# Placing TensorE's bursts in a fused attention and MoE kernel: empty sequencer instructions instead of split matmuls

## The chip, the cores and the metric

The kernel runs on one core of a Trainium2 chip. The metric is the device time of one execution in microseconds: the kernel before takes 282.03 us, the median of three runs (281.68 to 282.23).

## The reference

Two layers follow each other. The first is a linear attention with cosine weights over 8 batches, 8 heads, 576 positions and 64 columns a head; the second is a gated layer over the 4608 tokens that come out of it.

```python
# attention: q, k, v are [8, 8, 576, 64]
theta = pi / 2 * arange(576) / 576
phi(x) = concat([relu(x) * cos(theta), relu(x) * sin(theta)])     # 128 features
kv  = einsum('bhsf,bhfd', phi(k), v);  z = phi(k).sum(over positions)
x   = (phi(q) @ kv) / (phi(q) @ z + 1e-6)          # -> [4608, 512], heads side by side
# second layer: w_in [512, 2048], w_out [2048, 512], beta [2048]
h   = x @ w_in
out = (h * sigmoid(beta * h)) @ w_out
```

All inputs and the output are float32 in memory; the kernel's matmuls take bfloat16 and sum in float32.

## The kernel before

The attention is computed batch by batch (8 batches, b = 0 to 7), the second layer by chunks of 512 tokens (9 chunks, c = 0 to 8). While chunk c is in the second layer, batch c + 1 goes through the attention, in the gaps of the same program. The instructions of every engine are in the order in which the source gives them.

The attention of one batch has two stretches on TensorE that are made of many tiny matmuls. One is kv, 72 matmuls (L272 of the profile). The other is the numerators, 144 matmuls of 64 rows, 64 columns and 65 moved columns (L293). This text calls the second kind a burst. Each of TensorE's matmuls is a pair of instructions, a weight load and the matmul itself, so a burst is 288 instructions.

```python
def num_mm(b, n, jp, bank, slot):
    for cs in range(2):
        for jj in range(2):
            rows = slice(jj * HP, (jj + 1) * HP)
            for g in range(2):
                cols = slice(g * HP, (g + 1) * HP)
                nc.tensor.matmul(ps[cols, bank + jj, slot * E : (slot + 1) * E],
                                 lhsT=(qts[b % 2], qs_of(b))[cs][rows, jp, n, cols],
                                 rhs=kv[rows, g, jp, cs, :], start=(cs == 0), stop=(cs == 1))

def num_all(b, t, bank):            # three of these make one burst
    for i in range(3):
        for jp in range(2):
            num_mm(b, 3 * t + i, jp, bank, 2 * i + jp)
```

In the second layer, chunks 0 and 1 use plain products. From chunk 2 on the output, and from chunk 5 on also half of h, is computed by a scheme with seven products of half-size blocks instead of eight (names 1 to 7 in the code); it needs sums and differences of blocks of the operands, which VectorE makes. For h these are sums of weights (made once) and sums of x (made for each chunk):

```python
def x_sums(c):
    xt, n = xt_tile(c), NB // 2
    X11, X12, X21, X22 = (xt[:, i * n : (i + 1) * n, jp] for jp in range(2) for i in range(2))
    t1, t2, t3, t4 = (wx["x"][:, i] for i in range(4))
    nc.vector.tensor_tensor(t1, X12, X11, op=ALU.subtract)       # L458
    nc.vector.tensor_tensor(t2, X22, t1, op=ALU.subtract)        # L459
    nc.vector.tensor_tensor(t3, X22, X12, op=ALU.subtract)       # L460
    nc.vector.tensor_tensor(t4, X21, t2, op=ALU.subtract)        # L461
```

In three places a matmul can be split by columns into two of half the width, which computes the same and makes TensorE's program longer by two instructions. The splits serve nothing but that: they shift where in the program the bursts begin.

```python
def h_plain(c, jt, bank, cols=1):                     # plain half of h, chunks 5 to 8
    xt = xt_tile(c)
    w = NB // cols
    for mi in range(MI):                              # MI = 4
        jp, g = divmod(mi, 2)
        for o in range(0, NB, w) if mi else (0,):     # the first of four is never split
            z = o + w if mi else NB
            nc.tensor.matmul(ps[:, bank, o * 64 : z * 64], lhsT=win[...], rhs=xt[:, o:z, jp, ...], ...)

def o_mm(c, tt, jts, cols=1):                         # output of chunks 0 and 1
    ...
    for jt in jts:
        w = DM // cols if jt > 0 else DM              # jt = 0 is never split
        for m0 in range(0, DM, w):
            nc.tensor.matmul(o_ps[:, m0 : m0 + w], lhsT=gs[c, jt // 4][...], rhs=wout[:, jt, m0 : m0 + w], ...)

# inside o_fast: one of the seven products of the output, chunks 2 to 8
def prod(dst, left, right, start, stop, pieces=False):
    for i in order:                                   # 8 matmuls of 256 columns
        w = HM // 2 if i and pieces else HM
        for m in range(0, HM, w):
            nc.tensor.matmul(dst[:, m : m + w], lhsT=left(i), rhs=right[:, i, m : m + w], ...)
```

Which are split: in chunk 1's output those from slot 24 on (slots 16 to 31 are four parts of four matmuls for each of four groups of tokens); in chunk 5's output product 4 of the first half of the tokens and products 2, 5, 7, 3, 4 of the second; in chunk 6 all eight groups of `h_plain`.

The end of chunk 4, with the second half of its output (`y`), stands in the source like this. `v_half` scales v for the next batch; its fifth argument is the engine, VectorE if there is none. The digits are products on TensorE, `a2`, `a7`, `a3` additions on VectorE, `c1`, `c5`, `cu`, `c4` copies on ScalarE.

```python
        y["1"]()
        ...
        v_half(b + 1, 0, 0, 3)
        y["5"]()
        y["c5"]()
        v_half(b + 1, 1, 2, 3, "act")
        y["6"]()
        y["cu"]()
        y["2"]()
        y["a2"]()
        v_half(b + 1, 0, 3, 5)
        y["7"]()
        y["a7"]()
        v_half(b + 1, 0, 5, 7)
        y["3"]()
        y["a3"]()
        v_half(b + 1, 0, 7, 9)
        if c == FAST - 1:                 # FAST = 5
            x_sums(c + 1)
        v_half(b + 1, 1, 3, 9, "act")
        y["4"]()
        y["c4"]()
```

Product 4 adds to the block of PSUM that `a7` reads, so it waits for `a7`. Chunk 5 begins with `ORDER = "Y1 c1Y X5 X1 ..."`: Y1 is two matmuls on x itself, X5 the first product on a sum of x (t1), X1 again one on x. The numerators are the letter N, late in that order and after all products of h.

Of the kernel before, what the change touches and what calls it, by code (L numbers as in the profile page):

```python
# [22 lines left out]
def kernel(  # L23
# [14 lines left out]
    nc = tc.nc  # L38
# [145 lines left out]
    def xt_tile(c):  # L184
        if c not in xts:
            xts[c] = xt_pool.tile([P, NB, 2, P], BF16, name="xt", tag="xt")
        return xts[c]
# [33 lines left out]
    def tan_mul(eng, dst, src, n0, n1):  # L221
        return eng.tensor_tensor(  # L222
            dst.rearrange("q n (g p) -> q n g p", g=2), src.rearrange("q n (g p) -> q n g p", g=2),
            tanr[:, n0:n1].unsqueeze(2).to_broadcast([P, n1 - n0, 2, HP]), op=ALU.mult)
# [23 lines left out]
    def qs_of(b):  # L248
        return wx["q"] if b > 3 and b % 2 == 0 else qs_first
# [5 lines left out]
    def q_tan(b, jp, behind=None):  # L255
        got = tan_mul(nc.gpsimd, qs_of(b)[:, jp], qts[b % 2][:, jp], 0, NQ)

        if behind is not None:
            tc.add_manual_dep(got.ins, behind.ins.name,
                              mybir.DependencyInfo(mybir.DependencyClass.Sync, mybir.DependencyReason.DATA),  # L260
                              reason="GpSimd behind the sums")
# [66 lines left out]
    def num_all(b, t, bank):  # L328
# [81 lines left out]
    def h_group(c, jt):  # L410
        h_mm(c, jt)
        h_act(c, jt)

    def h_silu(c, jt, bank):
        if (c, jt // 4) not in gs:
            gs[c, jt // 4] = gt_pool.tile([P, 4, TCH], BF16, name="g_t", tag="g_t")
        nc.scalar.activation(gs[c, jt // 4][:, jt % 4], ps[:, bank], AF.Silu, scale=beta[:, jt : jt + 1])  # L417

    def h_plain(c, jt, bank, cols=1):
        xt = xt_tile(c)  # L420
        w = NB // cols
        for mi in range(MI):
            jp, g = divmod(mi, 2)
            for o in range(0, NB, w) if mi else (0,):
                z = o + w if mi else NB
                nc.tensor.matmul(ps[:, bank, o * 64 : z * 64], lhsT=win[jt // 4][:, mi, (jt % 4) * P : (jt % 4 + 1) * P],  # L426
                                 rhs=xt[:, o:z, jp, g * HP : (g + 1) * HP],
                                 start=(mi == 0), stop=(mi == MI - 1 and z == NB))
# [101 lines left out]
    def o_part(c, tt, part, cols=1):  # L530
        o_mm(c, tt, range(4 * part, 4 * part + 4), cols)
# [226 lines left out]
    def v_half(b, cs, n0=0, n1=NQ, eng="dve"):  # L758
        if b >= B:
            return  # L760
        v_scale(b, cs, n0=n0, n1=n1, eng=eng)
        if cs == 1 and n1 == NQ and b + 1 < B:
            load_raw(b + 1, "v")
# [11 lines left out]
    def x_part(b, t, bank):  # L775
        x_div(t, bank)
        x_turn_dma(b, 3 * t, 3 * t + 3)
# [51 lines left out]
    for slot in range(32):  # L829
        if slot < 16:  # L830
            h_group(1, slot)
        else:
            o_part(1, (slot - 16) // 4, slot % 4, 2 if slot > 23 else 1)
        one_unit(slot)

    def k_piece(b, j):
# [20 lines left out]
    H_COLS, O_COLS = {6: 8}, {5: ("4", "25734")}  # L857

    def x_sum(c, kind):
        xt, n = xt_tile(c), NB // 2  # L860
# [24 lines left out]
    def chunk(c, b, x, y, parts):  # L885
        steady = {"X": (0, 2, 0, 1), "Y": (4, 3, 4, 5), "Z": (8, 0, 2, 1), "V": (12, 4, 3, 5)}
        end = {"X": (0, 6, 0, 1), "E": (2, 5, 3, 4), "Y": (4, 2, 0, 1), "F": (6, 7, 3, 4), "Z": (8, 6, 0, 1),
               "V": (12, 5, 3, 4)}
        pairs = {n: h_fast(c, at[0], at[1:]) for n, at in (steady if b < B else end).items()}

        def plain_bank(n):
            return (2 if n == 7 else 6 + n % 2) if b < B else (2, 7)[n % 2]

        plain = [2, 3, 6, 7, 10, 11, 14, 15]
        outs = {"x": x, "y": y}

        def q_next():
            if b + 2 < B:
                q_turn_dma(b + 2)
                if b + 3 < B:  # L900
                    load_raw(b + 3, "q")

        def raw_next(name):
            if b + 2 < B:
                load_raw(b + 2, name)

        xs_all = {"x0", "x1", "x2"}
        take = prep(b, [
            ({"k0", "k1", "k2", "k3"} | xs_all, lambda: raw_next("k")),
            ({"q0", "q1"} | xs_all, q_next),  # L910
            ({f"{o}{n}" for o in "vw" for n in range(NQ)}, lambda: raw_next("v"))])
        last_sum = None
        for op in (ORDER if b < B else ORDER_END).split():
            n = int(op[-1]) if op[-1].isdigit() else None
            if op == "K":
                kv_mm(b, 0, 4)
                kv_mm(b, 1, 4)
            elif op == "kt":
                kv_take((0, 1), 4)
            elif op[0] == "N":  # L920
                for t, bank in enumerate(parts):
                    num_all(b, t, bank)
            elif op[0] == "x":
                x_part(b, n, parts[n])
                take(op)
            elif op[0] in "kvwq":
                take(op)
            elif op[0] == "t":
                if c + 1 < NTC:
                    x_sum(c + 1, n)  # L930
            elif op[0] == "g":
                if b + 1 < B:
                    q_tan(b + 1, n, None if n else last_sum)
            elif op[0] == "p":
                h_plain(c, plain[n], plain_bank(n), 2 if n < H_COLS.get(c, 0) else 1)
            elif op[:2] == "sp":
                h_silu(c, plain[n], plain_bank(n))
            elif op[0] == "o" and n is not None:
                outs[op[1]][op[2]]()
            elif op[0] == "o":  # L940
                outs[op[2]]["a" + op[1]]()
            elif op[0] == "c" and op[2] in "xyo":
                outs["x" if op[2] == "o" else op[2]][op[:2]]()
            elif op[0] == "s":
                last_sum = g_sum(c, 2 * int(op[1]), 2 * int(op[1]) + 2, n)
            else:
                pair = op[0] if op[0] in pairs else op[-1]
                pairs[pair][op.replace(pair, "")]()
# [24 lines left out]
    FAST = 5  # L973
    for c in range(2, NTC):
        b = c + 1
        parts = (6, 0, 4) if c < FAST else (0, 6, 4)
        cols = O_COLS.get(c, ("", ""))
        xb, yb = ((2, 3, 6), (1 if c == FAST - 1 else 7, 3, 6)) if c < FAST else ((3, 2, 0), (1, 2, 0)) if b < B else ((0, 3, 6), (1, 3, 6))
        x, y = o_fast(c, 0, xb, cols[0]), o_fast(c, 1, yb, cols[1])
        if c >= FAST:  # L980
            chunk(c, b, x, y, parts)
            continue
        sums = h_first(c)
        for t, bank in enumerate(parts):
            num_all(b, t, bank)
        q_tan(b + 1, 0, sums)
        q_tan(b + 1, 1)
        for i, n in enumerate("156273"):
            x[n]()
            if n in "156":  # L990
                x["c" + ("u" if n == "6" else n)]()
                x_part(b, i, parts[i])
        for j in range(4):
            k_piece(b + 1, j)
        for n in ("a7", "a2", "a3"):
            x[n]()
        att_q(b + 2)
        y["1"]()
        y["c1"]()
        v_half(b + 1, 1, 0, 1, "act")  # L1000
        x["4"]()
        x["c4"]()
        v_half(b + 1, 1, 1, 2, "act")
        v_half(b + 1, 0, 0, 3)
        y["5"]()
        y["c5"]()
        v_half(b + 1, 1, 2, 3, "act")
        y["6"]()
        y["cu"]()
# [6 lines that stand above are left out]
        y["3"]()  # L1016
        y["a3"]()
        v_half(b + 1, 0, 7, 9)
        if c == FAST - 1:
            x_sums(c + 1)  # L1020
        v_half(b + 1, 1, 3, 9, "act")
        y["4"]()
        y["c4"]()
# [30 lines left out]
```

## Time and profile before

| engine | busy us | share of the span |
|---|---|---|
| TensorE, matmuls | 272.2 | 97% |
| TensorE, weight loads (beside matmuls) | 192.4 | 69% |
| VectorE | 209.1 | 75% |
| ScalarE | 177.8 | 64% |
| GpSimd | 71.9 | 26% |

The profiled execution has a span of 279.6 us and 8687 instructions; TensorE's clock is at full speed throughout. The costliest lines of TensorE are L544 (products of the output, chunks 2 to 8), L378 (h of chunks 0 to 4), L521 (output of chunks 0 and 1), L426 (plain half of h, chunks 5 to 8) and L472 (products of h, chunks 5 to 8).

How to read it: matmuls are pipelined, so the length of one in the profile is longer than its share of TensorE's time; the time that a matmul takes from the engine is the difference between its start and the next one's. Busy shares say which engine is full. Idle time of an engine and its releaser say what it waited for, and "issue" means that the profile shows nothing it waited for. A queue of the kind "instruction" carries program text to an engine.

### The profile page before, as it was taken

How to read it: one execution, taken by the hardware profiler on the slowest of the kernel's cores; microseconds unless marked ns; L12 is line 12 of the kernel's file. 1: busy time of each engine (PE TensorE's matmuls, PEld its weight loads, DVE VectorE, ACT ScalarE, POOL GpSimd, SP SyncE). 2: the span in 40 equal slices, each digit the busy share in tenths (PEclk: the TensorE clock that was granted, in tenths of full speed). 3: DMA queues.
4: the chain of work that ended last, by engine and by line, in shares of the span. 5: the costliest groups of instructions: out<-in, count | busy, mean ns of one | idle time of the engine just before them, and what ended most of it. 6: DMA issues, size and time to landing. Idle time of an engine off the chain costs nothing.

```text
span 279.6 us, 8687 instructions
## 1 busy us (share of the span) xinstructions
PE 272.2 (97%) x3592; PEld 192.4 (69%) x3592; DVE 209.1 (75%) x539; ACT 177.8 (64%) x348; POOL 71.9 (26%) x89
## 2 busy tenths in 40 slices
PE   8999999999999999999999999999999999999993
PEld 8564455455674588548854886679888886888783
DVE  5989967669999586357749977799679779649832
ACT  5778756772137557675757585896685179529911
POOL 1444000633194074106320542007400140000000
PEclk9999999999999999999999999999999999999999
DMA  7999999999979959992899289407400540033006
GB/s 243 373 394 385 391 390 323 348 244 397 164 233 330 293 151 249 182 340 41 196 193 374 61 205 250 177 12 115 116 1 7 122 113 1 2 79 74 0 2 150
DMA packets 50583, 53.98 MB, mean 193 GB/s; under 512 B 31200, under 2 KB 31472, under 8 KB 50544
## 3 DMA queue, kind: packets, MB, share of 16 engines
q1 hardware_dynamic: 47584, 45.82, 58.0%
q0 software_dynamic: 2688, 7.34, 9.2%
q8 instruction: 28, 0.46, 0.7%
q10 hardware_dynamic: 272, 0.27, 0.4%
q14 instruction: 11, 0.09, 0.2%
HBM read 36.71 MB, written 9.44 MB: 165 GB/s over the span
## 4 chain that ended last, share of the span: by engine, by line
PE 89%; DMA 5%; DVE 3%; issue 1%; ACT 0%; ACTq 0%
PE ps L544 30%; PE ps L378 22%; PE ps L472 11%; PE ps L521 8%; PE ps L426 7%; DMA raw_q<-in_q_dram 5%; PE ps L293 4%; PE ps L272 3%; PE ps L602 1%; PE ps L234 1%; PE ps L606 1%; DVE xs L315 1%; DVE vb L219 0%; PE ps L616 0%; PE ps L352 0%
## 5 line engine op out<-in xcount | busy, mean ns | idle before, releaser
L378 PE MATMUL ps<-xt,win 128*128 128x512 bf16 (+1 forms) x324 | 71.1, 377 | 0.1
L386 ACT ACTIVATE g_t<-ps,beta 128x512 bf16<-128x512 f32 x80 | 54.6, 688 | 19.2 <-PE ps L378 17.9
L378 PEld LDWEIGHTS <-win 128*128 128x128 bf16 x324 | 31.1, 98 | 35.4 <-issue 0.2
L514 POOL DMA_DIRECT2D out_dram<-o_sb x56 | 32.7, 590 | 66.6 <-DVE o_sb L595 34.3
L544 PEld LDWEIGHTS <-S 128*128 128x128 bf16 x469 | 44.2, 98 | 4.8
L417 ACT ACTIVATE g_t<-ps,beta 128x512 bf16<-128x512 f32 x64 | 41.2, 696 | 3.4 <-PE ps L426 2.2
L544 PEld LDWEIGHTS <-g_t 128*128 128x128 bf16 x357 | 32.9, 98 | 3.7
L222 POOL TENSOR_TENSOR qs<-qt,tanr 128x1152 bf16<-128x1152 bf16 x8 | 18.9, 2387 | 48.5 <-DVE S L397 17.6
L397 DVE TENSOR_TENSOR S<-g_t 128x512 bf16<-128x512 bf16 (+1 forms) x62 | 22.3, 393 | 11.5 <-ACT g_t L386 9.1
L521 PE MATMUL ps<-wout,g_t 128*128 128x512 bf16 (+1 forms) x158 | 29.2, 339 | 0.0
L544 PE MATMUL ps<-wout,g_t 128*128 128x256 bf16 (+1 forms) x231 | 28.1, 270 | 0.0
L544 PE MATMUL ps<-wout,S 128*128 128x256 bf16 (+1 forms) x238 | 27.4, 266 | 0.0
L544 PE MATMUL ps<-T,S 128*128 128x256 bf16 (+1 forms) x231 | 27.1, 269 | 0.0
L426 PE MATMUL ps<-xt,win 128*128 128x512 bf16 (+1 forms) x120 | 24.0, 336 | 0.0
L315 DVE TENSOR_TENSOR xs<-ps,rden 128x768 bf16<-128x768 f32 (+4 forms) x26 | 22.8, 883 | 0.8
L219 DVE TENSOR_SCALAR vb<-raw_v,cos 128x256 bf16<-128x256 f32 x63 | 22.9, 421 | 0.2 <-DMA raw_v<-in_v_dram 0.2
L521 PEld LDWEIGHTS <-g_t 128*128 128x128 bf16 x158 | 15.0, 98 | 11.0
L217 ACT ACTIVATE vb<-raw_v,sin 128x256 bf16<-128x256 f32 (+1 forms) x50 | 21.8, 499 | 0.8 <-DMA raw_v<-in_v_dram 0.8
L472 PE MATMUL ps<-w_stage 128*128 128x256 bf16 x120 | 20.3, 273 | 0.4 <-DVE w_stage L458 0.4
L472 PEld LDWEIGHTS <-w_stage 128*128 128x128 bf16 x160 | 15.5, 98 | 4.2 <-issue 0.5
L222 POOL TENSOR_TENSOR w_stage<-qt,tanr 128x1152 bf16<-128x1152 bf16 x4 | 9.5, 2380 | 26.1 <-DVE den L304 26.1
L426 PEld LDWEIGHTS <-win 128*128 128x128 bf16 x120 | 11.7, 98 | 6.3
(104 smaller groups left out, 384.9 us busy)
## 6 DMA issues: line engine op xcount, KB each, us to landing
raw_v<-in_v_dram SPq DMA_DIRECT2D x7, 1152.0 KB, 10.9
raw_k<-in_k_dram SPq DMA_DIRECT2D x7, 1152.0 KB, 8.4
raw_q<-in_q_dram SPq DMA_DIRECT2D x7, 1152.0 KB, 7.8
out_dram<-o_sb POOLq DMA_DIRECT2D x56, 128.0 KB, 5.2
w_stage<-in_moe_w_in_dram SPq DMA_DIRECT2D x3, 1024.0 KB, 13.3
w_stage<-in_moe_w_out_dram SPq DMA_DIRECT2D x2, 1024.0 KB, 8.4
w_stage<-in_moe_w_out_dram SPq DMA_DIRECT2D x4, 512.0 KB, 12.0
out_dram<-o_sb SPq DMA_DIRECT2D x13, 128.0 KB, 2.4
```

The lines of the kernel that those rows point to most:

```text
L219: nc.vector.tensor_scalar(o, a, scalar1=t[:, n : n + 1], scalar2=None, op0=ALU.mult)
L222: return eng.tensor_tensor(dst.rearrange("q n (g p) -> q n g p", g=2), src.rearrange("q n (g p) -> q n g p", g=2), tanr[:, n0:n1].unsqueez ...
L315: nc.vector.tensor_tensor(o.rearrange("q j n s d -> q j (n s) d"), nv[:, :, a:z, :, 0:D].rearrange("q j n s d -> q j (n s) d"), rden[:, :, ...
L378: nc.tensor.matmul(ps[:, h_bank(c, jt), blocks.start * 64 : blocks.stop * 64], lhsT=win[jt // 4][:, mi, (jt % 4) * P : (jt % 4 + 1) * P], ...
L386: nc.scalar.activation(gs[c, jt // 4][:, jt % 4], ps[:, h_bank(c, jt)], AF.Silu, scale=beta[:, jt : jt + 1])
L397: return nc.vector.tensor_tensor(o, l, r, op=op)
L417: nc.scalar.activation(gs[c, jt // 4][:, jt % 4], ps[:, bank], AF.Silu, scale=beta[:, jt : jt + 1])
L426: nc.tensor.matmul(ps[:, bank, o * 64 : z * 64], lhsT=win[jt // 4][:, mi, (jt % 4) * P : (jt % 4 + 1) * P], rhs=xt[:, o:z, jp, g * HP : (g ...
L472: nc.tensor.matmul(dst, lhsT=left[:, g], rhs=right[:, :, g * HP : (g + 1) * HP], start=start and g == 0, stop=stop and g == 1, skip_group_ ...
L514: eng.dma_start(out=out_v[bb, n][:, m0:m1], in_=o_sb[hf * HP : (hf + 1) * HP, m0:m1])
L521: nc.tensor.matmul(o_ps[:, m0 : m0 + w], lhsT=gs[c, jt // 4][:, jt % 4, tt * P : (tt + 1) * P], rhs=wout[:, jt, m0 : m0 + w], start=(jt == ...
L544: nc.tensor.matmul(dst[:, m : m + w], lhsT=left(i), rhs=right[:, i, m : m + w], start=start and i == 0, stop=stop and i == order[-1], skip ...
```

## The change

It has three parts. First, the splits in chunks 5 and 6 go, and in their place 137 empty instructions (nops) are put into TensorE's program ahead of chunk 5; a nop computes nothing and takes one place in the program where a split matmul adds two. Second, chunk 1's output is split from slot 19 on, not from slot 24. Both are for the places at which the bursts begin. Third, the four sums of x for chunk 5 are given earlier in chunk 4, so that they are there when chunk 5 asks for them. What is computed stays the same. The table PADS holds two counts for a chunk, ahead of the chunk and after its burst; only the first of chunk 5 is not zero.

```diff
+    def pad(c, n):
+        for _ in range(PADS.get(c, (0, 0))[n]):
+            nc.tensor.nop(hint="pad", nofuse=True)
...
-            o_part(1, (slot - 16) // 4, slot % 4, 2 if slot > 23 else 1)
+            o_part(1, (slot - 16) // 4, slot % 4, 2 if slot > 18 else 1)
...
-    H_COLS, O_COLS = {6: 8}, {5: ("4", "25734")}
+    PADS = {5: (137, 0)}
...
-                h_plain(c, plain[n], plain_bank(n), 2 if n < H_COLS.get(c, 0) else 1)
+                h_plain(c, plain[n], plain_bank(n))
...
     for c in range(2, NTC):
         ...
-        cols = O_COLS.get(c, ("", ""))
+        pad(c, 0)
         ...
-        x, y = o_fast(c, 0, xb, cols[0]), o_fast(c, 1, yb, cols[1])
+        x, y = o_fast(c, 0, xb), o_fast(c, 1, yb)
...
         y["5"]()
         y["c5"]()
+        if c == FAST - 1:
+            x_sums(c + 1)
         v_half(b + 1, 1, 2, 3, "act")
...
         v_half(b + 1, 0, 7, 9)
-        if c == FAST - 1:
-            x_sums(c + 1)
         v_half(b + 1, 1, 3, 9, "act")
```

(Left out: a second call of `pad` after the numerators, which places nothing with this table.)

More of the change, by code (lines that the diff above doesn't have):

```diff
@@ L922, in chunk @@
                     num_all(b, t, bank)
+                pad(c, 1)
             elif op[0] == "x":
@@ L985 @@
             num_all(b, t, bank)
+        pad(c, 1)
         q_tan(b + 1, 0, sums)
```

## The prediction

> **What bounds the kernel now.** I read the busy shares first, then the chain that ended last, then who waited on TensorE, then the timeline at the places where TensorE stood still. Shares and chain of the page:
>
> ```profile
> PE 272.2 (97%) x3592; PEld 192.4 (69%) x3592; DVE 209.1 (75%) x539; ACT 177.8 (64%) x348; POOL 71.9 (26%) x89
> ...
> PE 89%; DMA 5%; DVE 3%; issue 1%; ACT 0%; ACTq 0%
> ...
> q8 instruction: 28, 0.46, 0.7%
> ```
>
> TensorE is 97% busy and 89% of the chain, so nothing on another engine counts unless TensorE waits for it. The third line is the queue that brings TensorE its program: 28 packets, 0.46 MB, 16 KB each. I need it below.
>
> The waits of TensorE alone come to three microseconds (columns: who waited for whom, us in total, times, longest). The first, third and fifth lines lie in the first 20 us, which the change does not touch:
>
> ```profile
> PE ps L602 <- DVE zero_b L149: 1.0, 1, 1.0
> PE ps L293 <- issue: 0.9, 2, 0.5
> PE ps L293 <- ACT kv L282: 0.5, 1, 0.5
> PE ps L472 <- DVE w_stage L458: 0.4, 1, 0.4
> PE ps L234 <- DVE qb L194: 0.2, 1, 0.2
> ```
>
> Two of these lines bear on the change. The second is a pair of stops on "issue": TensorE waited for nothing that the profile shows. The fourth is a stop for VectorE's sums of x. On the timeline they look like this (start, length, instruction, idle time before it, which is counted from the modelled end of the last matmul and so is shorter than the step between starts):
>
> ```profile
> 97.42 0.22 PE L293 MATMUL ps<-kv,qt 64*64 64x65 bf16 x4
> 98.06 0.23 PE L293 MATMUL ps<-kv,qs 64*64 64x65 bf16 x4 [0.43 <-issue]
> ...
> 127.42 0.19 PE L293 MATMUL ps<-kv,qt 64*64 64x65 bf16 x1 [0.48 <-issue]
> ...
> 168.64 0.38 PE L472 MATMUL ps<-xt,win 128*128 128x256 bf16 x2
> 169.37 0.38 PE L472 MATMUL ps<-w_stage 128*128 128x256 bf16 x2 [0.35 <-DVE w_stage L458]
> ```
>
> Both "issue" stops lie inside a burst of 144 tiny matmuls (the numerators, one burst for each batch from batch 2 on). Elsewhere a matmul follows the last one every 216 ns (512 columns), 109.2 ns (256) or 55.8 ns (128), by differences of start times, with no wait between. There is little else to win.
>
> [...] 28 packets of 16,384 bytes, and 28 x 256 = 7,168 beside 7,189 TensorE instructions in the program. [...] No nop is in this trace. [...] the trace records each of TensorE's 19 semaphore instructions at 51 ns. [...] the burst of batch 5 sends 288 instructions in 1.36 us, 4.7 ns each.
>
> **Why the bursts stop.** I numbered TensorE's instructions in the built program and put the trace's matmuls beside them. Both stops fall at one place of a 256-block: after instructions 2734 and 3501, which is 256k + 174 and + 173. So a block boundary lies at 256k + 175. [...] a burst covers 256 instructions in 1.2 us[...]. For batch 3, packet start 95.50 to resumption 98.06 is 2.6 us; for batch 4 125.01 to 127.42, 2.4 us. A place below is the boundary's distance from the burst's first instruction; minus means ahead of it.
>
> Before, batches 2 to 7: -19/237, **24/280**, **7/263**, -10/246, -75/181, -16/240. Only those with both boundaries inside stopped: bursts of 1.98 and 2.03 us beside 1.36 us, so 0.62 and 0.67 us lost. The edge lies between -10 and +7.
>
> **The change part by part.**
>
> Splits. A split matmul costs 2 x 109.2 - 216 = 2.4 ns (or 2 x 55.8 - 109.2 = 2.4 ns) and adds two instructions. Removed: 24 in chunk 6's products of h (8 groups, 3 of 4 matmuls each) and 42 in chunk 5's output (6 products, 7 of 8 each): 66 x 2.4 = 0.16 us less. Added: chunk 1's output is split from slot 19, not 24: 4 + 15 = 19 more, 0.05 us. Net **-0.11 us**.
>
> Bursts 3 to 5. The 19 splits push everything later by 38 instructions: places become -14/242, -31/225, -48/208. All are on the side that ran clean. **-1.29 us** (0.62 + 0.67).
>
> Bursts 6 and 7. Without the two old sets of splits and with 137 nops, the places are 6/262 and -59/197. Burst 7 is safe. Burst 6 comes within one instruction of where batch 4 stopped (7/263). What may save it is how far the sequencer runs ahead: at its semaphore instructions the trace shows it 17 or 33 instructions in front of the array, and 33 would carry it over the first boundary early enough. I charge half a stop: **+0.3 us**.
>
> Sums of x. In chunk 5 the third matmul starts 624 ns after the second instead of 109 ns: 0.515 us lost to VectorE's four sums, 0.42 us each (L458 to L461, 168.90 to 170.44). They now come after three products of v. On the timeline of VectorE there is a hole just there:
>
> ```profile
> 166.28 0.42 DVE L594 TENSOR_TENSOR o_sb<-ps,p 128x256 f32<-128x256 f32 x1 [1.72 <-ACT vb L217]
> ```
>
> 1.72 us idle, from 164.56; four sums take about 1.6 us. Their input landed long before (the transpose issued at 158.2, 2.8 us to landing). So they fit, and **-0.5 us**.
>
> The nops. 137 empty instructions stand between chunk 4's last matmul and chunk 5's first. The sequencer can't reach them early: chunk 4's last product (eight matmuls, from 167.77) waits for VectorE's addition, which ends at 167.57, and the trace has the first sequencer instruction of chunk 5 at 167.65. The array then has work until 168.64, so **0.99 us** is hidden, 7.2 ns for each nop. If nops pass at the burst's 4.7 ns, they take 0.65 us and cost nothing. If each takes the 51 ns of a semaphore instruction, they take 7.0 us and 6.0 us shows. No view decides this, because no nop ran. For the fast side: the sequencer hands over 16 instructions in under 0.1 us here[...]. [...] I choose the fast side at 6 in 10.
>
> Sum, fast nops: -0.11 - 1.29 + 0.3 - 0.5 = -1.6, so 280.4 us; some tenths for nops that stick out give **280.9 us**. Sum, slow nops: 280.4 + 6.0 = 286.4 us.
>
> **The rivals.**
> 1. *The nops become the bound at one place*: TensorE idle for 3 to 9 us at 168.6. For it: 51 ns recorded for TensorE's semaphore instructions, and twice (3.45 and 16.56 us) the next load began 77 ns after one. Against it: these carry a wait, nops do not. Time 284 to 290 us.
> 2. *Burst 6 takes over the stop of burst 4*: for it, the place 6/262; against it, a sequencer 33 ahead. It would give back 0.65 us: 280.8 with free nops.
> 3. *The stops move with conditions the profile doesn't hold*[...], so that repeated runs lose less than the trace shows. Then the first 1.3 us is smaller and the time is 281.5.
> 4. *The sums come too early*: if their tile were late, VectorE would stall ahead of the additions that free the banks. The landing at 161.0 speaks against it; no change in time.
>
> **Range and chances.** Fast nops give 279.8 to 281.5, slow ones 284 to 290. A range of 279.8 to 288.0 takes the first whole and most of the second. Faster by 2% means 276.4, more than all stops together yield: 0.01. Slower by 2% means 287.7: 137 x t - 1.0 above 7.3, so nops of about 61 ns or more: 0.17. Within 2%: 0.82.
>
> **What would show it.** Right: no "issue" stop at bursts 3 and 4; no stop for the sums at chunk 5; the sums in the hole at 164.6; the start of chunk 5 right behind chunk 4's last matmul. Wrong: a hole between L544 and L472 near 167 us, whose length plus 0.99 us, divided by 137, is the price of a nop; an "issue" stop of about 0.6 us in burst 6. The step I trust least is the price of a nop; if the prediction fails, it fails there.

## The result, and the profile after

The changed kernel takes **291.86 us** (median of six runs, 289.96 to 292.63) beside 282.10 us: a ratio of **1.034** (95% interval 1.030 to 1.038). It is slower by 9.8 us, above the 288.0 us at which the predicted range ended.

Busy shares and chain of the page, and the row of TensorE's granted clock in forty slices:

```profile
PE 272.1 (94%) x3539; PEld 191.3 (66%) x3545; DVE 209.5 (72%) x539; ACT 178.0 (61%) x348; POOL 70.6 (24%) x89
...
PEclk9999999999999999999999985999999999999999
...
PE 86%; DMA 6%; issue 3%; DVE 2%; SPq 1%; ACT 1%; ACTq 0%; DVEq 0%
```

TensorE does the same work (272.1 us busy against 272.2) in a span of 289.7 us instead of 279.6. Three per cent of the chain are now "issue", and there is a dip of the clock at two thirds of the span that was not there before. TensorE's own waits after:

```profile
PE ps L476 <- issue: 9.0, 1, 9.0
PE ps L272 <- DVE rk L194: 1.2, 2, 1.0
PE ps L606 <- DVE zero_b L149: 1.0, 1, 1.0
PE ps L272 <- ACT rk L192: 0.9, 1, 0.9
PE ps L293 <- ACT kv L282: 0.5, 1, 0.5
PE ps L525 <- issue: 0.2, 1, 0.2
```

The two stops on "issue" at L293 and the one for the sums are gone from this list, as they were meant to be. In their place is one stop of 9.0 us. The timeline of TensorE around it, and the row that the profile has for the source line of the nop:

```profile
167.14 1.04 PE L548 MATMUL ps<-T,g_t 128*128 128x256 bf16 x8
177.21 0.59 PE L476 MATMUL ps<-xt,win 128*128 128x256 bf16 x2 [9.04 <-issue]
...
178.45 1.91 PE L430 MATMUL ps<-xt,win 128*128 128x512 bf16 x4
...
L421 PEldq NOP  x137: 13/13/13, 167.0 to 177.0; - x137
```

The hole lies between chunk 4's last product and chunk 5's first. The nops run from 167.02 to 177.05 us. Each is *recorded* as 13 ns long, but they start 71 ns apart (105 of the 136 steps; the mean is 73.6 ns), so 137 of them take 10.0 us. Busy time of these instructions would have misled: 137 x 13 ns is 1.8 us. What counts is the step from one to the next. Of the 10.0 us the array still had work for 1.0 us (the next matmul would have been due at 168.02); 9.2 us shows, by the step between starts.

The third of these lines is slow as well: four matmuls of 512 columns in 1.91 us by the modelled ends, and 427 ns from start to start instead of 216. The clock record has half speed from 171.31 us, which is 3.3 us after the array ran dry, to 181.55 us. The matmuls that ran in it, 177.21 to 181.55, lost 2.1 us.

The sums went into VectorE's idle time; in place of 1.72 us there is 0.26 us left ahead of the same addition:

```profile
164.98 0.42 DVE L465 TENSOR_TENSOR w_stage<-xt,w_stage 128x512 bf16<-128x512 bf16 x1
165.65 0.42 DVE L598 TENSOR_TENSOR o_sb<-ps,p 128x256 f32<-128x256 f32 x1 [0.26 <-ACT vb L217]
```

Sum over the two traces: +9.2 (hole) + 2.1 (half clock) - 0.5 (sums) - 0.4 (burst 3, which still stopped for 0.23) - 0.7 (burst 4) - 0.1 (splits) = +9.6, beside 10.05 us between the spans. Of the 0.45 us that are left, 0.3 us was lost before burst 2 (it starts at 68.72 us instead of 68.41), ahead of everything that the change touches.

### The profile page after: what moved, and what is told of

Read it like the earlier page. It is cut to its first block, busy times and chain, and to the rows that moved or that the text cites. A ratio compares the mean times of both kernels' runs of the same rounds, so it can differ in the third digit from the quotient of the medians.

```text
span 289.7 us, 8724 instructions
## 1 busy us (share of the span) xinstructions
PE 272.1 (94%) x3539; PEld 191.3 (66%) x3545; DVE 209.5 (72%) x539; ACT 178.0 (61%) x348; POOL 70.6 (24%) x89
## 4 chain that ended last, share of the span: by engine, by line
PE 86%; DMA 6%; issue 3%; DVE 2%; SPq 1%; ACT 1%; ACTq 0%; DVEq 0%
PE ps L548 27%; PE ps L378 24%; PE ps L476 11%; PE ps L525 10%; PE ps L430 7%; PE ps L293 4%; DMA raw_v<-in_v_dram 3%; PE ps L272 3%; DMA raw_k<-in_k_dram 2%; SPq L79 1%; DVE xs L315 1%; ACT vb L217 0%; PE ps L352 0%; DVE win L115 0%; PE ps L234 0%
## 5 line engine op out<-in xcount | busy, mean ns | idle before, releaser
L378 PE MATMUL ps<-xt,win 128*128 128x512 bf16 (+1 forms) x324 | 71.1, 377 | 0.1
L518 POOL DMA_DIRECT2D out_dram<-o_sb x56 | 31.6, 571 | 65.6 <-DVE o_sb L599 33.0
L548 PEld LDWEIGHTS <-g_t 128*128 128x128 bf16 x336 | 32.5, 98 | 3.9
L548 PE MATMUL ps<-wout,g_t 128*128 128x256 bf16 x224 | 28.1, 273 | 0.0
L548 PE MATMUL ps<-wout,S 128*128 128x256 bf16 x224 | 27.4, 273 | 0.0
L548 PE MATMUL ps<-T,S 128*128 128x256 bf16 x224 | 27.1, 273 | 0.0
L430 PE MATMUL ps<-xt,win 128*128 128x512 bf16 x96 | 24.9, 390 | 0.0
L476 PE MATMUL ps<-xt,win 128*128 128x256 bf16 x80 | 15.0, 283 | 9.0 <-issue 9.0
L525 PEld LDWEIGHTS <-g_t 128*128 128x128 bf16 x177 | 16.9, 98 | 9.2
L476 PE MATMUL ps<-w_stage 128*128 128x256 bf16 x120 | 21.0, 280 | 0.0
```

The costliest lines, as they stand in the source:

```text
L378: nc.tensor.matmul(ps[:, h_bank(c, jt), blocks.start * 64 : blocks.stop * 64], lhsT=win[jt // 4][:, mi, (jt % 4) * P : (jt % 4 + 1) * P], ...
L476: nc.tensor.matmul(dst, lhsT=left[:, g], rhs=right[:, :, g * HP : (g + 1) * HP], start=start and g == 0, stop=stop and g == 1, skip_group_ ...
L518: eng.dma_start(out=out_v[bb, n][:, m0:m1], in_=o_sb[hf * HP : (hf + 1) * HP, m0:m1])
L525: nc.tensor.matmul(o_ps[:, m0 : m0 + w], lhsT=gs[c, jt // 4][:, jt % 4, tt * P : (tt + 1) * P], rhs=wout[:, jt, m0 : m0 + w], start=(jt == ...
```

## The experiments

Three theories were tried. **A**: a nop costs some 73 ns of TensorE's sequencer, in a row, and the hole also halves the clock. **B**: the new places of the bursts cost the time. **C**, formed on the way: a stop at a block boundary can also come behind a burst. Every ratio is against the kernel before, run on the same chip beside it. Three chips were used, on which that kernel took 281.81, 281.50 and 281.66 us, so medians of different experiments compare only roughly.

| kernel | median us | ratio (95% interval) |
|---|---|---|
| changed, no nops | 280.35 | 0.9961 (0.9945 to 0.9977) |
| changed, 13 nops in a row | 281.18 | 0.9983 (0.9966 to 1.0000) |
| changed, 40 in a row | 283.10 | 1.0042 (1.0027 to 1.0056) |
| changed, 137 spread | 279.89 | 0.9932 (0.9910 to 0.9953) |
| 40 in a row, 97 spread | 282.14 | 1.0030 (1.0013 to 1.0047) |
| 68 in a row, 69 spread | 286.29 | 1.0176 (1.0150 to 1.0202) |
| no nops, no splits | 285.31 | 1.0071 (1.0039 to 1.0103) |
| 13 nops behind burst 6 | 281.82 | 1.0011 (0.9996 to 1.0026) |
| before, sums moved | 281.00 | 0.9982 (0.9962 to 1.0003) |
| before, splits from slot 19 | 280.58 | 0.9970 (0.9958 to 0.9982) |
| before, both of these | 280.15 | 0.9945 (0.9929 to 0.9960) |
| changed, 13 spread | 280.94 | 0.9989 (0.9967 to 1.0011) |

**1. The nops away.**

```diff
-    PADS = {5: (137, 0)}
+    PADS = {}
```

> The changed kernel with the table of nops empty; everything else stays. Theory A (a nop costs about 73 ns of TensorE's sequencer, one after the other, and the hole that they make also halves the clock for a while): the hole of 9.2 us and the 2.1 us of slow matmuls after it both go, so about 280.4 us, 1.6 us under the kernel before. Theory B (the loss comes from the new places of the bursts, which the split matmuls had kept well): bursts 6 and 7 now begin with a boundary at 143 and 78 and stop, so about 0.6 us each stays and most of the 10 us with them: over 285 us.

Measured 280.35 us. The nops account for the whole loss; the "over 285 us" of B did not come. Taking the nops out also moves bursts 6 and 7; experiment 3 holds these in place. The trace has no wait of TensorE after the first 30 us, with bursts 6 and 7 at 143 and 78.

**2. Fewer nops, in the same place.** `PADS = {5: (13, 0)}` and `{5: (40, 0)}`.

> 13 nops ahead of chunk 5 instead of 137. Theory A: 13 x 73 ns = 0.95 us, which is what the array still has queued there (0.9 to 1.0 us), so no hole and the time of the kernel without nops, within 0.2 us. Rival (the array stops for any nop, whatever is queued): 0.95 us more than without nops.

> 40 nops ahead of chunk 5. Theory A: 40 x 73 ns = 2.9 us, of which 0.9 to 1.0 us is hidden: a hole of 1.9 to 2.0 us, too short for the clock to fall (in the changed kernel it fell 3.3 us after the array had stopped), so 1.9 us more than without nops. Rival[...]: about the same 9 us as with 137.

Measured 0.8 and 2.75 us above the kernel without nops, against 0 and 1.9 expected. Both misses have one cause, and it is not the nops. With 13 the trace has no hole at chunk 5, so they were hidden. It has a stop elsewhere, behind burst 7 (timeline of TensorE):

```profile
212.59 0.82 PE L548 MATMUL ps<-T,S 128*128 128x256 bf16 x6
214.18 0.81 PE L548 MATMUL ps<-T,S 128*128 128x256 bf16 x6 [0.77 <-ACT p L595]
```

From start to start 0.94 us are lost there. ScalarE's copy is named as the releaser, yet the kernel without nops, whose program differs by the 13 nops alone, loses only 0.06 us behind this burst. The nops moved burst 7 from 78 to 65. With 40 nops (burst 7 at 38) the trace has the hole of 2.06 us that A asks for, 1.04 us behind burst 7, and 0.78 us in burst 3. So theory C: what counts is the time between two block boundaries. With one at 65 in the burst, the next comes 33 instructions behind its end.

**3. The same nops, spread, and the dose at fixed places.** One nop behind each of 25 matmuls of h and 112 of the output in chunk 4:

```diff
+                if c == 4:                       # in each product of the output
+                    nc.tensor.nop(hint="pad", nofuse=True)
...
+            if c == 4 and 16 <= 4 * jt + mi < 41:   # in h
+                nc.tensor.nop(hint="pad", nofuse=True)
...
-    PADS = {5: (137, 0)}
+    PADS = {}
```

> The same 137 nops, and so the same places of bursts 6 and 7 (6/262 and -59/197), but one behind each of 137 matmuls of chunk 4 (25 of 512 columns, which take 216 ns each, 112 of 256 columns, 109 ns each). Theory A: the sequencer needs about 73 + 10 ns for a nop and the pair after it, less than the matmul takes, so nothing shows: the time of the kernel without nops, within 0.4 us. Rival (a nop makes the array run dry[...], wherever it is): 137 x 73 ns = 10 us or more on top.

Measured 279.89 us, the lowest median of all (its interval overlaps that of the kernel without nops), and 12 us below the same 137 nops in a row. The program is as long and all bursts from 6 on stand where they stand in the changed kernel. So theory B falls for good: at the same places of bursts 6 and 7, single nops behind busy matmuls cost nothing that shows, and 137 in a row cost 12 us. The trace shows no stop after the first 30 us, not even at burst 6 (6/262).

Then part of the 137 in a row ahead of chunk 5, the rest spread:

```diff
-    PADS = {5: (137, 0)}
+    PADS = {5: (40, 0)}          # and 97 spread;  (68, 0) and 69 spread
```

> 40 nops in a row ahead of chunk 5 and the other 97 one by one behind matmuls of chunk 4, so that all bursts stand where they stand in the changed kernel (6/262, -59/197). Theory A (73.6 ns for each nop in a row, some 0.9 us of queue to hide it): a hole of 2.0 us in the profile and 2.0 us more than with all 137 spread (279.89), so about 281.9 us. Rival (the extra 0.8 us that 13 nops and the 2.75 us that 40 nops cost without the spread ones are the price of the nops, with nothing hidden): 2.8 us more, 282.7 us.

> 68 nops in a row and 69 spread, places as before. Theory A: 68 x 73.6 = 5.0 us, less 0.9 hidden, a hole of 4.1 us. That is longer than the 3.3 us after which the clock fell in the changed kernel, so the clock should fall to half and cost some more, 0.5 to 2 us: 284.5 to 286 us. Rival (the clock plays no part, only nops count): 284.0 us and full clock in the profile.

The holes are as expected, 2.07 and 4.14 us between starts (40 x 73.6 = 2.9 and 68 x 73.6 = 5.0, less 0.9). In time, 40 cost 2.25 us by the medians and 2.8 by the ratios, with an interval too wide to tell A's 2.0 from the rival's 2.8; the trace tells it. A line of each timeline:

```profile
169.66 0.38 PE L476 MATMUL ps<-xt,win 128*128 128x256 bf16 x2 [1.90 <-DMA raw_k<-in_k_dram]
```

```profile
172.30 0.38 PE L476 MATMUL ps<-xt,win 128*128 128x256 bf16 x2 [3.98 <-issue]
...
173.16 1.91 PE L430 MATMUL ps<-xt,win 128*128 128x512 bf16 x4
```

The first is a warning on releasers: it names a transfer, but the last nop ends at 169.50 us, 0.16 us before the matmul. The second shows the clock: with 68 the four wide matmuls take 1.91 us as in the changed kernel, and the record has half speed for 3.41 us. With 40 it stays full. So 68 cost 6.4 us by the medians, 4.1 of them the hole. The clock's part is about 1.7 us (half of 3.41) by that record, and the trace also has 0.54 us in burst 3. The 286.29 us lie just above A's 284.5 to 286 and well above the rival's 284.0. In the changed kernel, after a hole of 9.2 us, the half speed lasted 10.24 us, three times the 3.41 us here.

**4. Nops where nothing is queued.** `PADS = {5: (0, 13)}`, behind burst 6:

> 13 nops in a row behind burst 6 instead of ahead of chunk 5; burst 7 keeps the place 65 that it had with 13 nops in front (281.18). Behind a burst the array has next to nothing queued: Theory A expects a hole of 0.8 to 0.95 us there, and about 0.9 us more than with the 13 nops in front, 282.0 us. Rival (nops are hidden at any place by the sequencer's lead of 17 to 33 instructions): the same 281.2 us.

```profile
184.96 0.81 PE L548 MATMUL ps<-wout,g_t 128*128 128x256 bf16 x6 [0.70 <-issue]
```

From the start of the burst's last matmul to the start of the next one it takes 0.89 us, instead of 0.13 us without nops. So 0.77 us shows of the 0.95 us that 13 x 73 ns make, a little less than A's 0.8 to 0.95. Only 0.2 us is hidden behind a burst; ahead of chunk 5 all but 0.05 us was. In time it is 0.6 us more than 13 in front by the medians and 0.8 by the ratios, nearer to A's 0.9 than to the rival's none. The stop behind burst 7 was 0.51 us in this trace.

**5. No splits either.**

```diff
-            o_part(1, (slot - 16) // 4, slot % 4, 2 if slot > 18 else 1)
+            o_part(1, (slot - 16) // 4, slot % 4, 1)
...
-    PADS = {5: (137, 0)}
+    PADS = {}
```

> No nops and no split matmul anywhere, sums of x early: bursts 3 to 7 get the places 84, 67, 50, -15/241, -80/176. Rule of the prediction (a stop only where both boundaries lie inside the burst): no stop, 0.12 us under the kernel without nops, 280.2 us or less. Theory C (what counts is the time between two boundaries, and the second may also lie up to some 40 instructions behind the burst; 13 nops alone showed a stop of 0.94 us with a place of 65, right behind burst 7): stops of up to 1 us behind bursts 4 and 5, perhaps 3, so 281 to 283 us.

Slower than before, though it has the fewest instructions of all: by 0.7% by the ratio, which is of the seven shorter of its thirteen executions, and by 3.8 us (1.4%) by the median of all (285.31 beside 281.50 us). The prediction's rule fails. C was right on where the stops are and too low on what they cost. TensorE's waits, and the longest of them on the timeline:

```profile
PE ps L548 <- issue: 4.0, 3, 2.6
...
100.08 0.38 PE L548 MATMUL ps<-wout,g_t 128*128 128x256 bf16 x2
103.06 0.82 PE L548 MATMUL ps<-wout,g_t 128*128 128x256 bf16 x3 [2.60 <-issue]
```

All three stand behind bursts (3, 4 and 5, with boundaries at 84, 67 and 50); between starts they cost 2.76, 0.63 and 1.13 us. The first cost more than its length. The clock record goes to half at 102.89 us, before TensorE resumes, and back at 106.30; the 16 matmuls that started in it lost 1.6 us. So a hole of 2.76 us was enough here, and the clock fell 2.59 us after the array ran dry (100.30 us), sooner than the 3.29 us in the changed kernel; the 2.07 us of experiment 3 left the clock full. A mean clock of 0.993 or 0.994 was recorded in all seven executions from 285.31 us up, which fits one such stretch of 3.41 us each (an estimate from this trace: 3.41 x 0.5 / 283.7 = 0.6% missing).

**6. The place alone.** 13 nops, each behind a matmul of chunk 4, so that only bursts 6 and 7 move:

> The changed kernel with 13 nops, each behind a matmul of chunk 4, where nops were hidden, so that only the places move: bursts 6 and 7 to 130 and 65. Theory C (the place alone makes the stop behind burst 7): a stop of 0.5 to 1 us behind burst 7, and about the 281.2 us that 13 nops in a row cost, against 280.35 without nops. Rival (nops in a row cost that 0.8 us by themselves): 280.2 us, no stop behind burst 7.

Measured 280.94 us, between the rival's 280.2 and the 281.2 of 13 in a row; the stop behind burst 7 is there but only 0.18 us in the trace. By the intervals it can't be told from either. That the place makes a stop is supported (65 three times: 0.94, 0.51, 0.18 us; 78: 0.06 us), but its size is not fixed.

The packets of queue 8, of kind "instruction" (28 of 16,384 bytes before and after; 27 in the kernel without nops), show in the same traces what the stop goes with. The blocks of 256 instructions are read from the traces too: the two stops of the kernel before are 767 instructions apart, three times 256 less one. The times are us from the start of each trace, at the two boundaries those of the weight load there:

| kernel, burst | place | first boundary | packet starts | second boundary | stop there |
|---|---|---|---|---|---|
| before, 4 | 7/263 | 125.64 | 125.01 | 127.42 | 0.67 |
| before, sums moved, 4 | 7/263 | 125.39 | 123.81 | 126.48 | none |
| changed, 13 in a row, 7 | 65/321 | 210.31 | 211.87 | 214.18 | 0.94 |
| changed, 13 spread, 7 | 65/321 | 210.57 | 211.25 | 213.69 | 0.18 |
| no nops, no splits, 3 | 84/340 | 96.41 | 100.79 | 103.06 | 2.76 |

At one and the same place, the later the packet starts after the first boundary, the longer the stop. From the packet's start to the second boundary it is 2.27 to 2.67 us in all five rows. Over all fourteen traces, 25 stops of 0.07 us or more (by the starts of weight loads) stand at a second boundary (to within two instructions), in a burst or behind it, and TensorE goes on 2.27 to 2.71 us after the packet's start; where it passed one without a stop, the packet had started at least 2.39 us before. So what these stops go with is the time from the packet's start to the second boundary, of which the time between two boundaries is only a part. Why a packet starts late is not shown, nor why TensorE goes on waiting behind it: at burst 4 of the kernel before the packet took 1.06 us, and TensorE went on 1.35 us after its end. In the last row the DMA engines were full between the boundary and the packet's start (share 0.94 and 1.02 in its two halves); whether that delays a packet was not tested.

**7. The change's other parts alone, on the kernel before.**

> The kernel before with the sums of x moved, nothing else. The prediction's term: the stop of 0.515 us at the start of chunk 5 goes, so 0.5 us less than before (ratio 0.998). Rival (the chain closes up elsewhere: the time the array waits there is taken by the next wait): no change.

> The kernel before with chunk 1's output split from slot 19 on, nothing else. The prediction's term: bursts 3 and 4 leave the places 24/280 and 7/263 for -14/242 and -31/225, and their stops of 0.62 and 0.67 us go: 1.3 us less, ratio 0.9955. Rival (the stops vary from run to run, and at -14/242 burst 3 still stops now and then, 0.2 to 0.8 us in traces so far): 0.5 to 1 us less, ratio 0.997 to 0.998.

> Both of the above, so the changed kernel with its old split matmuls and no nops; bursts 6 and 7 at 143 and -54/202. If the two terms add up, the sum of the two gains, 1.2 to 1.8 us less than before, and 0.16 us more than the changed kernel without nops or splits (280.35): about 280.3 us.

The sums bring 0.5 us (0.18%, with an interval that just includes none), and their stop is gone from the trace. The splits bring 0.85 us (0.30%, interval 0.18 to 0.42), not 1.3, as the rival said. Together they bring 1.55 us, which is a little more than their sum (1.35) and within the intervals.

## Why the prediction was wrong, point by point

- **The price of a nop is the step that failed.** The prediction put two prices beside each other, 4.7 and 51 ns, chose the fast one at 6 in 10, and so 0 us for the nops. Measured were 73.6 ns: more than either. The prediction's own check (hole plus 0.99 us, by 137) gives (9.2 + 0.99) / 137 = 74 ns. The better reading was in its text as a rival: twice in the trace before, the next load began 77 ns after a semaphore instruction. I took the recorded 51 ns for the slow price, where the step to the next instruction was the measure. The fast price, 4.7 ns, was measured on matmuls and loads alone; that a nop would pass like them was my estimate, and no trace had shown it.
- **What was hidden was right**: 0.99 us predicted, 1.0 measured. So was the place of the hole.
- **The half clock was missing.** 2.1 us, in no term of the sum. Even the slow branch (286.4 us) came out too low for both reasons: 280.35 + 9.2 + 2.1 = 291.65, the measured 291.86 within its spread.
- **The sum without nops was right, in part by luck**: 280.4 predicted, 280.35 measured, but two of its terms were off and made up for each other. The bursts brought 0.85 us and not 1.29. Burst 3 at -14/242 is no clean place: it lost 0.23, 0.34, 0.54, 0.78 and 0.87 us in five of eleven traces, 0.1 us in two and less in the others. And the stops of the kernel before vary as well: with the sums moved, burst 3 lost 0.33 us at 24/280 and burst 4 nothing at 7/263. Which of the two weighs more is not shown. Burst 6 at 6/262, charged with 0.3 us, lost at most 0.07 us in the four kernels that have it there.
- **The rule of the places was too narrow.** "Both boundaries inside the burst" fits the trace before. It leaves out that the second boundary may lie behind the burst (experiments 2 and 5) and that the packet starts at different times (experiment 6). So "burst 7 is safe" was said of the right place for an incomplete reason. The prediction's 2.6 and 2.4 us from a packet's start to resumption lie within the 2.27 to 2.71 us of the 25 stops; what happens in that time was not shown.
- **Rival 1 was the outcome**, just beyond the upper end of what it was given (9.2 us idle for 3 to 9, 291.86 us for 284 to 290); rival 3 (stops that vary) is true beside it.

## What to carry to other kernels

Before an instruction is put on a full engine because it "does nothing", price it by the step from its start to the next one's, and ask what is queued ahead of it at that place: one nop behind each matmul was free here, 137 in a row cost 12 us. A hole in a full TensorE cost more than its length where the clock fell to half: about 1.7 us on top of 4.14 us, 1.6 us on top of 2.76 us. An edit that only adds or drops instructions can cost time far from where it stands: 13 nops ahead of chunk 5, hidden there, went with a stop of 0.94 us behind burst 7, 46 us later. Compare such edits with the places held fixed, and in more than one trace.

## What the runs showed of the hardware

- A nop on TensorE's sequencer is recorded at 13 ns and takes 71 to 74 ns in a row, about fifteen times the 4.7 ns at which matmuls and loads pass in a burst (288 in 1.36 us).
- A stop at a second block boundary ended 2.27 to 2.71 us after the start of the packet of 16,384 bytes before it (25 stops in fourteen traces). At one place (-14/242) such stops came to anything from nothing to 0.87 us in eleven traces.
- After a hole of 2.76 us the clock was at half for 3.41 us, after one of 4.14 us for 3.41 us, after one of 9.2 us for 10.24 us; after 2.07 us it stayed full.
